# Sigmoid attention and a swish layer on one core: a new order for the opening, new tables for the visits, other cuts at the end

## The chip, the core and the metric

The kernel runs on one NeuronCore of a Trainium2 chip. The core has TensorE (PE: matmuls; its loads of weights are listed apart as PEld), VectorE (DVE), ScalarE (ACT), GpSimd (POOL) and SyncE (SP). Here GpSimd issues the loads (and does a few products), SP issues the first loads and all stores. The metric is the time of one execution on the device, in microseconds; the time before is a median of three runs. All other times are counted from the start of the profiled span.

## The reference

The inputs are `q`, `k`, `v` of shape (8, 12, 448, 64), `w_in` (768, 2048), `w_out` (2048, 768) and `beta` (2048).

```python
scores = matmul(q, k.transpose(0, 1, 3, 2)) / sqrt(64) - log(448)
attn   = 1 / (1 + exp(-scores))                  # a sigmoid, no softmax
x      = matmul(attn, v)                         # to (8 * 448, 12 * 64) = (3584, 768)
h      = x @ w_in                                # (3584, 2048): "first layer"
g      = h / (1 + exp(-beta * h))
out    = g @ w_out                               # (3584, 768): "second layer"
```

## The kernel before, in words

**Groups and visits.** The 12 heads of a batch form three groups of four (`g` = 3 * batch + group; 24 in all). A group's q and k are loaded as fp16 and transposed on VectorE (`transpose`, L208 for q, L217 and L221 for k). A visit (`visit`) is the scores of one group against 128 keys: 8 matmuls of 448 columns (`score`, L237) into two PSUM score tiles of two banks each, then one sigmoid over all four banks on ScalarE (`weigh_two`, L265). The 64 keys left over of two groups share one visit, with 16 matmuls. So the next visit's scores wait until ScalarE has read all four banks. `attend` ("values", L340) multiplies the weights by v, and VectorE copies the result to `xTs` (L349).

**Dense work.** `dense1` (L362) is the first layer of batches 0 and 1: six matmuls per 128 hidden columns, a sigmoid with `beta` (L374), a product on VectorE (L377) into `gt`. The later batches go through `blocks` (L531 and others) between the visits of one window and the next. The second layer is `dense2` (L392), `strassen` (L651, on pairs of 128-token tiles, with sums of hidden columns on VectorE, L638, and adds of results, L669) and `single` (L445, one tile alone). These matmuls form one list, `fill`, and are taken from it one after the other.

**Order.** Every engine executes in the order in which the kernel writes its instructions (`manual_schedule`). In the opening, the list `BEGIN` sets it item by item: `("scores", g, half, second)` is half a group's queries against two key tiles (`second` 0) or the rest (`second` 1), each with two sigmoids (L250); `("idle", n)` is n matmuls on zeros (L820, 256 columns); `("k", g)`, `("q", g, half)` are transposes; `("v", 0)` doubles the leftover keys' v (L171); `("values", g, half)`; `("beta",)` transposes beta (L834); `("dense", n)` takes n matmuls from `fill`. In this stretch there are three score tiles, from `("two",)` on two. `LOADS` is the order of the loads on GpSimd's queue; `("loads",)` puts the list `LATER` behind it. All later waits in the queue follow this order.

After `BEGIN`, a loop over `visits` follows. Each visit is followed by as many dense matmuls as the rest of the list divided by the visits left, plus `MORE[n]` matmuls for visit n. `LATE[n]` says behind how many of them the values of the group before come. Visit 0 is the first of group 3.

**The end.** The last tile of 128 tokens is done alone: its right half of 384 columns first (L445, copied by VectorE, L413), then the left half in two pieces of `QUART` = 192 columns, 16 matmuls each; ScalarE copies each piece (L407) and SP stores it (L703). `store` cuts the stores of the last batch only at the ends of tiles and of the batch.

Of the kernel before, what the change touches and what calls it, by code (L numbers as in the profile page):

```python
# [13 lines left out]
def kernel(  # L14
# [14 lines left out]
    B, H, S, D = q.shape  # L29
    NTOK, DM = out.shape  # L30
    DFF = moe_w_in.shape[1]
    P = 128
# [12 lines left out]
    HALF = DM // 2  # L45
# [36 lines left out]
    def touch(i: int):  # L82
        used[i] = max(used.values(), default=0) + 1

    def bank(cols: int = S, hold=None, at=None):
        if at is None:
            at = min((i for i in used if i not in held.values()), key=used.get)
        assert at not in held.values()
        touch(at)
        if hold is not None:  # L90
            held[hold] = at
        width[at] = cols
        return ps[:, at, 0:cols]
# [287 lines left out]
    m2s = {}  # L381
    left = {}
    def release(key):
        touch(held.pop(key))
        m2s.pop(key)

    def dense2(t: int, half: int, dc: int):

        if dc == 0:
            m2s[t, half] = bank(HALF, (t, half))  # L390
        m2 = m2s[t, half]
        nc.tensor.matmul(  # L392
            m2,
            gt[:, dc, cols(t)],
            w_out16[:, dc, half * HALF : (half + 1) * HALF],
            start=(dc == 0),
            stop=(dc == NDC - 1),
        )
        if dc == NDC - 1:
            leave(t, half, m2)  # L400

    def leave(t: int, half: int, m2, piece=None):
        lo, hi = half * HALF, (half + 1) * HALF
        if piece is not None:
            release((t, half, piece))
            lo, hi = lo + piece * QUART, lo + (piece + 1) * QUART
            nc.scalar.copy(out=osbs[t][:, lo:hi], in_=m2)  # L407
            store(t, lo, hi)
            return
        release((t, half))  # L410
        if t not in osbs:
            osbs[t] = outp.tile([P, DM], FP32, tag="osb", name="osb")
        nc.vector.tensor_copy(out=osbs[t][:, lo:hi], in_=m2)  # L413
        left[t] = left.get(t, 0) + 1
        if t == NT - 1:
            store(t, lo, hi)
        elif left[t] == 2:
            store(t, 0, DM)

    QUART = HALF // 2  # L420

    def sum_of_halves(t: int):
        sums[t, 0] = sump.tile([P, ND, P], FP16, tag="sum", name="sum")
        nc.vector.tensor_tensor(out=sums[t, 0], in0=hid(t, 0), in1=hid(t, 1), op=ALU.add)

    def single(t: int, n: int, dc: int, piece=None):

        if (n, dc) == (0, 0):
            if (t, 0) not in sums:
                sum_of_halves(t)  # L430
            for half in range(1 + (t < NT - 1)):
                m2s[t, 1 - half] = bank(HALF, (t, 1 - half))
        if piece is not None and (n, dc) == (1, 0):
            m2s[t, 0, piece] = bank(QUART, (t, 0, piece))
        both = sums[t, 0]
        half, x, w = (
            (1, hid(t, 0), B12),
            (0, hid(t, 1), B21),
            (1, both, B22),
            (0, both, B11),  # L440
        )[n]
        m2 = m2s[(t, half) if piece is None else (t, half, piece)]
        stop = n > 1 and dc == ND - 1
        w = w[:, dc] if piece is None else w[:, dc, piece * QUART : (piece + 1) * QUART]
        nc.tensor.matmul(m2, x[:, dc], w, start=(n < 2 and dc == 0), stop=stop)  # L445
        if stop:
            leave(t, half, m2, piece)

    NT = NTOK // P
# [165 lines left out]
    def hid(t: int, half: int):  # L615
        return gt[:, half * ND : (half + 1) * ND, cols(t)]
# [23 lines left out]
    def strassen(t: int, i: int, dc: int):  # L640
# [45 lines left out]
        elif i == 6:  # L686
            add(o1[:, L], a, o1[:, L], ALU.subtract)
            release((t, "a"))
            store(t, 0, DM)

    def store(t: int, lo: int, hi: int):
        osb = osbs[t]
        c, end = t * P, (t + 1) * P
        while c < end:
            b, i = divmod(c, S)
            rows = out[b * S : (b + 1) * S, lo:hi]
            if b == B - 1:
                n = min(end - c, S - i)
                to = rows[i : i + n]
            else:  # L700
                n = BLK
                to = rows.rearrange("(p c) m -> c p m", c=NB)[i // BLK]
            nc.sync.dma_start(out=to, in_=osb[c - t * P : c - t * P + n, lo:hi])  # L703
            c += n
# [10 lines left out]
    def alone(t: int):  # L715
        order = [(n, None) for n in range(4)]
        if t == NT - 1:
            order = [(0, None), (2, None), (1, 0), (3, 0), (1, 1), (3, 1)]
        for n, piece in order:
            for dc in range(ND):  # L720
                yield M2_US, lambda a=(t, n, dc, piece): single(*a), n < 3
# [41 lines left out]
    with tc.manual_schedule():  # L763
        def load(what, *a):
# [15 lines left out]
                load_w_out(*a)  # L780

        LOADS = [
            ("q", 1, 0), ("k", 1), ("k", 2), ("q", 2, 0), ("v", 0, 3), ("last",), ("q", 1, 1), ("q", 2, 1),
            ("q", 0, 1), ("w_in", 0, 2), ("w_in", 2, 4), ("w_in", 4, 6), ("w_in", 6, 8), ("w_in", 8, 10),
            ("w_in", 10, 12), ("w_in", 12, 14), ("w_in", 14, 16),
        ]
        LATER = [
            ("qk", 3), ("w_out", 0, 0), ("w_out", 1, 0), ("values", 1), ("qk", 4), ("qk", 5), ("w_out", 0, 1),
# [27 lines left out]
        idle = bank(512)  # L816
# [13 lines left out]
        def beta_columns():  # L830
# [4 lines left out]

        BEGIN = [
            ("cast", 1, 0, 8, False), ("cast", 1, 8, 14, True), ("cast", 0, 0, 7, True), ("k", 0), ("q", 0, 0),
            ("q", 1, 0), ("idle", 20), ("scores", 0, 0, 1), ("k", 1), ("idle", 1), ("idle", 4), ("idle", 2),
            ("k", 2), ("q", 2, 0), ("scores", 1, 0, 0), ("idle", 9), ("v", 0), ("scores", 1, 0, 1),
            ("scores", 0, 0, 0), ("idle", 7), ("scores", 2, 0, 0), ("values", 0, 0), ("q", 1, 1),  # L840
            ("scores", 2, 0, 1), ("beta",), ("q", 0, 1), ("values", 1, 0), ("scores", 0, 1, 0),
            ("values", 2, 0), ("scores", 0, 1, 1), ("dense", 6), ("scores", 1, 1, 1), ("two",), ("dense", 9),
            ("loads",), ("scores", 1, 1, 0), ("q", 2, 1), ("dense", 21), ("scores", 2, 1, 0), ("dense", 12),
            ("values", 0, 1), ("scores", 2, 1, 1), ("values", 1, 1), ("values", 2, 1), ("dense", 45), ("k", 3),
            ("q", 3, 0), ("q", 3, 1), ("dense", 33),
        ]
        for what, *a in BEGIN:
            if what == "q":
# [44 lines left out]
        def left_us(n: int):  # L893
# [2 lines left out]
        AV_US = 1.5  # L896
        GLANCE = 3
        MORE = {
# [3 lines left out]
        }  # L902
        RESERVE = (1.99, 3.28)
        LATE = {
            0: 1, 17: 1, 26: 6, 34: 4, 45: 2, 48: 3, 68: 10, 72: 10,
        }
        turns = {4 * QPB: 1, 6 * QPB: 1}
        first = [next(i for i, x in enumerate(visits) if x[0] == g) for g in range(QPB, NQUAD)]
# [118 lines left out]
```

## Time and profile before

| what | us |
|---|---|
| median of 3 runs (lowest, highest) | 374.64 (374.45, 375.24) |
| the profiled execution: time, span | 374.53, 372.8 |
| busy: TensorE | 366.1 |
| busy: ScalarE | 260.0 |
| busy: VectorE | 254.4 |
| last matmul ends / last copy ends / last store issued | 369.5 / 369.9 / 370.2 |

The busy time of TensorE contains matmuls that overlap, with modelled ends, and the 43 matmuls on zeros; starts of matmuls tell more than ends. In a row of the timeline, the two numbers are start and length, both in microseconds, of consecutive instructions of one kind (x says how many), and the bracket holds the engine's idle time just before and what ended it. In the waits of an engine, the three numbers are the total in microseconds, how often, and the longest. In the chain, a share is part of the span of the work that ended last, followed back.

### The profile page before, as it was taken

Reading aid. Unit: us, or ns where it says so; the run is one execution under the profiler, and the core shown is the slowest. Engines: PE = TensorE matmul, PEld = TensorE weight load, DVE = VectorE, ACT = ScalarE, POOL = GpSimd, SP = SyncE. Lnnn points to the kernel's source line nnn. Section 1 sums busy time; section 2 is a strip of 40 time slices with the busy share of each in tenths; the row PEclk is TensorE's granted clock in tenths of the full one; section 3 lists DMA queues with packets and bytes.
Section 4 is the critical chain, followed back from the end, with each engine's and each line's share of the span. In section 5 each row is a group of like instructions: output and inputs, shape, how many; then the busy total and the mean of one; then the engine's idle time right before and its main releaser. Section 6 shows DMA issues by size and latency. Waiting matters only on the chain.

```text
span 372.8 us, 7315 instructions
## 1 busy us (share of the span) xinstructions
PE 366.1 (98%) x2907; PEld 185.1 (50%) x2907; DVE 254.4 (68%) x479; ACT 260.0 (70%) x311; POOL 90.4 (24%) x136
## 2 busy tenths in 40 slices
PE   8899999999999999999999999999999999999996
PEld 5466544443444455544444445554444455555664
DVE  4335786776586966787666767778767667679671
ACT  5995766698967668887777749887678647883000
POOL 7833343141151013234133003235100002230000
PEclk9999999999999999999999999999999999999999
DMA  9999999993369030029829410018903111000333
GB/s 171 177 195 203 198 204 198 218 124 51 51 85 174 1 86 1 2 49 128 165 38 218 103 24 21 3 30 113 164 4 86 42 44 42 3 0 1 86 84 128
DMA packets 42546, 34.65 MB, mean 93 GB/s; under 512 B 21888, under 2 KB 38928, under 8 KB 42512
## 3 DMA queue, kind: packets, MB, share of 16 engines
q0 software_dynamic: 36688, 22.47, 44.5%
q1 hardware_dynamic: 5824, 11.71, 10.9%
q8 instruction: 23, 0.38, 0.4%
q14 instruction: 11, 0.09, 0.1%
HBM read 45.62 MB, written 11.01 MB: 152 GB/s over the span
## 4 chain that ended last, share of the span: by engine, by line
PE 89%; ACT 5%; DVE 2%; DMA 1%; issue 1%; POOL 0%; ACTq 0%; POOLq 0%
PE ps L531 26%; PE ps L651 25%; PE ps L237 11%; PE ps L340 10%; PE ps L362 9%; PE ps L392 4%; PE ps L445 4%; ACT attns L265 2%; ACT attns L250 2%; DMA raw<-in_k_dram 1%; ACT sg L374 1%; DVE xT L349 0%; DVE qT L208 0%; DVE kT L217 0%; ACT osb L672 0%
## 5 line engine op out<-in xcount | busy, mean ns | idle before, releaser
L265 ACT ACTIVATE attns<-ps,nlogs 128x1792 f16<-128x1792 f32 x75 | 131.7, 1756 | 41.1 <-PE ps L237 40.1
L651 PEld LDWEIGHTS <-sum 128*128 128x128 f16 x440 | 40.4, 98 | 37.0 <-issue 12.1
L545 POOL TENSOR_TENSOR gt<-attns,sg 128x448 f16<-128x448 f32 x21 | 23.9, 1139 | 141.6 <-ACT sg L542 141.6
L237 PE MATMUL ps<-qT,kT 32*128 32x448 f16 (+3 forms) x864 | 52.3, 341 | 2.1 <-ACT attns L250 1.1
L542 ACT ACTIVATE sg<-ps,beta_sb 128x448 f32<-128x448 f32 x72 | 45.3, 633 | 8.4 <-PE ps L531 5.9
L531 PE MATMUL ps<-xT,w_in 128*128 128x448 f16 x216 | 49.2, 353 | 0.0
L531 PE MATMUL ps<-xT,w_S 128*128 128x448 f16 x216 | 49.2, 352 | 0.0
L651 PE MATMUL ps<-w_T,sum 128*128 128x384 f16 x264 | 48.5, 327 | 0.0
L545 DVE TENSOR_TENSOR gt<-ps,sg 128x448 f16<-128x448 f32 x72 | 44.3, 619 | 3.9 <-ACT sg L542 3.7
L349 DVE CAST xT<-ps 128x448 f16<-128x448 f32 (+1 forms) x54 | 28.9, 568 | 19.8 <-PE ps L340 19.8
L531 PEld LDWEIGHTS <-w_in 128*128 128x128 f16 x288 | 28.0, 98 | 26.6 <-issue 0.7
L340 PE MATMUL ps<-attns,v 128*64 128x448 f16 (+3 forms) x432 | 40.6, 340 | 0.1
L669 DVE TENSOR_TENSOR osb<-ps,osb 128x384 f32<-128x384 f32 x55 | 30.5, 555 | 14.4 <-PE ps L651 12.6
L362 PE MATMUL ps<-xT,w_in 128*128 128x448 f16 (+1 forms) x240 | 39.8, 316 | 0.1
L638 DVE TENSOR_TENSOR sum<-gt 128x1024 f16<-128x1024 f16 x55 | 36.5, 680 | 0.2
L377 DVE TENSOR_TENSOR gt<-ps,sg 128x448 f16<-128x448 f32 (+1 forms) x40 | 20.0, 528 | 22.6 <-ACT sg L374 22.5
L126 POOL DMA_DIRECT2D raw<-in_q_dram x26 | 14.5, 560 | 81.0 <-DVE kT L221 75.1
L651 PE MATMUL ps<-w_out,gt 128*128 128x384 f16 x176 | 33.4, 327 | 0.0
L651 PE MATMUL ps<-w_out,sum 128*128 128x384 f16 x176 | 32.2, 327 | 0.0
L591 DVE TENSOR_TENSOR ps<-ps,attns 128x448 f32<-128x448 f32 x24 | 15.2, 633 | 23.3 <-PE ps L531 20.0
L531 PEld LDWEIGHTS <-w_S 128*128 128x128 f16 x216 | 21.1, 98 | 19.4
L362 PEld LDWEIGHTS <-w_in 128*128 128x128 f16 x240 | 21.9, 98 | 16.8 <-issue 5.6
(54 smaller groups left out, 377.0 us busy)
## 6 DMA issues: line engine op xcount, KB each, us to landing
out_dram<-osb SPq DMA_DIRECT2D x100, 96.0 KB, 2.2
raw<-in_k_dram POOLq DMA_DIRECT2D x23, 224.0 KB, 5.6
raw<-in_q_dram POOLq DMA_DIRECT2D x21, 224.0 KB, 3.8
v<-in_v_dram POOLq DMA_DIRECT2D x32, 144.0 KB, 6.2
w_in<-in_moe_w_in_dram POOLq DMA_DIRECT2D x8, 384.0 KB, 10.4
w_out<-in_moe_w_out_dram POOLq DMA_DIRECT2D x4, 768.0 KB, 13.8
v<-in_v_dram POOLq DMA_DIRECT2D x16, 48.0 KB, 6.1
out_dram<-osb SPq DMA_DIRECT2D x2, 384.0 KB, 2.3
```

The lines of the kernel that those rows point to most:

```text
L237: nc.tensor.matmul(sco[base : base + nk, hh, u0 : u0 + n], kT[g][lo : lo + BLK, jt * P : jt * P + nk, e], qT[g][lo : lo + BLK, c0 : c0 + n ...
L265: nc.scalar.activation(out=attns[:, slot : slot + 2].rearrange("p n h s -> p (n h) s"), in_=sco, func=AF.Sigmoid, bias=nlogs[:, 0:1], scal ...
L340: nc.tensor.matmul(av[hh * D : (hh + 1) * D, 0:n], vs[b][base : base + nk, 2 * (s % NPAIR) + hh, jt], at[base : base + nk, hh, 0:n], start ...
L349: nc.vector.tensor_copy(out=xTs[b][:, s % NPAIR, c0 : c0 + n], in_=av[:, 0:n])
L362: nc.tensor.matmul(m1, w_in16[:, hc, dc * P : (dc + 1) * P], xTs[b][:, hc, c0 : c0 + n], start=(hc == 0), stop=(hc == NHC - 1),)
L377: nc.vector.tensor_tensor(out=gt[:, dc, off : off + n], in0=m1, in1=sg[:, 0:n], op=ALU.mult)
L531: nc.tensor.matmul(out, w[:, c, i * P : (i + 1) * P], m[:, c], start=(start and c == 0), stop=(c == KH - 1), skip_group_check=not start,)
L542: nc.scalar.activation(out=sg, in_=h, func=AF.Sigmoid, bias=0.0, scale=beta_sb[:, dc : dc + 1])
L545: return lambda: engine.tensor_tensor(out=gt[:, dc, b % 2 * S : b % 2 * S + S], in0=h, in1=sg, op=ALU.mult)
L638: nc.vector.tensor_tensor(out=sums[t, i], in0=x, in1=y, op=op)
L651: nc.tensor.matmul(m2, (x if op is None else sums[t, i])[:, dc], w[:, dc], start=first, stop=(dc == ND - 1), skip_group_check=i >= 4,)
L669: nc.vector.tensor_tensor(out=out, in0=in0, in1=in1, op=op)
```

## The change

In the opening, the two visits of group 0's first half of queries stand next to each other, with 4 of the matmuls on zeros between them; the later such matmuls are set 2, 2, 8 and 6 (before: 1, 4, 2, 9 and 7). Beta is transposed ahead of the doubling of v instead of after the third group's scores. The loads of v's leftover keys move ahead of group 2's q, group 0's second half of q goes ahead of group 2's, and the last two slices of `w_in` swap. The dense matmuls between the later scores change from 6, 9, 21, 12, 45, 33 to 12, 6, 21, 9, 39, 45; `loads` comes one step later. `MORE` and `LATE` have other entries. At the end the left half is cut into 256 and 128 columns, and the stores of the last batch, but for the last tile, take at most 48 rows.

```diff
-            lo, hi = lo + piece * QUART, lo + (piece + 1) * QUART
+            lo, hi = CUTS[piece : piece + 2]
...
-    QUART = HALF // 2
+    CUTS = (0, 2 * P, HALF)
...
-            m2s[t, 0, piece] = bank(QUART, (t, 0, piece))
+            m2s[t, 0, piece] = bank(CUTS[piece + 1] - CUTS[piece], (t, 0, piece))
...
-        w = w[:, dc] if piece is None else w[:, dc, piece * QUART : (piece + 1) * QUART]
+        w = w[:, dc] if piece is None else w[:, dc, CUTS[piece] : CUTS[piece + 1]]
...
+    ROWS = 48
+
     def store(t: int, lo: int, hi: int):
...
-                n = min(end - c, S - i)
+                n = min(end - c, S - i, P if t == NT - 1 else ROWS)
...
         LOADS = [
-            ("q", 1, 0), ("k", 1), ("k", 2), ("q", 2, 0), ("v", 0, 3), ("last",), ("q", 1, 1), ("q", 2, 1),
-            ("q", 0, 1), ("w_in", 0, 2), ("w_in", 2, 4), ("w_in", 4, 6), ("w_in", 6, 8), ("w_in", 8, 10),
-            ("w_in", 10, 12), ("w_in", 12, 14), ("w_in", 14, 16),
+            ("q", 1, 0), ("k", 1), ("k", 2), ("last",), ("q", 2, 0), ("v", 0, 3), ("q", 1, 1), ("q", 0, 1),
+            ("q", 2, 1), ("w_in", 0, 2), ("w_in", 2, 4), ("w_in", 4, 6), ("w_in", 6, 8), ("w_in", 8, 10),
+            ("w_in", 10, 12), ("w_in", 14, 16), ("w_in", 12, 14),
         ]
...
         BEGIN = [
             ("cast", 1, 0, 8, False), ("cast", 1, 8, 14, True), ("cast", 0, 0, 7, True), ("k", 0), ("q", 0, 0),
-            ("q", 1, 0), ("idle", 20), ("scores", 0, 0, 1), ("k", 1), ("idle", 1), ("idle", 4), ("idle", 2),
-            ("k", 2), ("q", 2, 0), ("scores", 1, 0, 0), ("idle", 9), ("v", 0), ("scores", 1, 0, 1),
-            ("scores", 0, 0, 0), ("idle", 7), ("scores", 2, 0, 0), ("values", 0, 0), ("q", 1, 1),
-            ("scores", 2, 0, 1), ("beta",), ("q", 0, 1), ("values", 1, 0), ("scores", 0, 1, 0),
-            ("values", 2, 0), ("scores", 0, 1, 1), ("dense", 6), ("scores", 1, 1, 1), ("two",), ("dense", 9),
-            ("loads",), ("scores", 1, 1, 0), ("q", 2, 1), ("dense", 21), ("scores", 2, 1, 0), ("dense", 12),
-            ("values", 0, 1), ("scores", 2, 1, 1), ("values", 1, 1), ("values", 2, 1), ("dense", 45), ("k", 3),
-            ("q", 3, 0), ("q", 3, 1), ("dense", 33),
+            ("q", 1, 0), ("idle", 20), ("scores", 0, 0, 1), ("idle", 4), ("scores", 0, 0, 0), ("k", 1),
+            ("idle", 2), ("k", 2), ("q", 2, 0), ("idle", 2), ("scores", 1, 0, 0), ("beta",), ("idle", 8),
+            ("scores", 1, 0, 1), ("v", 0), ("idle", 6), ("scores", 2, 0, 0), ("values", 0, 0), ("q", 1, 1),
+            ("scores", 2, 0, 1), ("q", 0, 1), ("values", 1, 0), ("scores", 0, 1, 0),
+            ("values", 2, 0), ("scores", 0, 1, 1), ("dense", 12), ("scores", 1, 1, 1), ("two",), ("dense", 6),
+            ("scores", 1, 1, 0), ("loads",), ("q", 2, 1), ("dense", 21), ("scores", 2, 1, 0), ("dense", 9),
+            ("values", 0, 1), ("scores", 2, 1, 1), ("values", 1, 1), ("values", 2, 1), ("dense", 39), ("k", 3),
+            ("q", 3, 0), ("q", 3, 1), ("dense", 45),
         ]
...
         MORE = {
-            0: -2, 2: 1, 3: -1, 5: 1, 10: 1, 13: 1, 14: -2, 15: 1, 16: -1, 17: -2, 19: -1, 20: -2, 24: -1,
-            27: -1, 28: -1, 32: -1, 34: 1, 35: 1, 43: -1, 44: 1, 45: 1, 46: -1, 47: 1, 49: 1, 51: 1, 52: 2,
-            53: -1, 54: 1, 55: 1, 59: 1, 67: -1,
+            0: -1, 2: 1, 3: -4, 8: -3, 9: 1, 10: 1, 12: 2, 13: 1, 14: -2, 15: 1, 16: -1, 17: -2, 19: -1, 20: -2,
+            25: -2, 27: -1, 28: -1, 32: -1, 34: 1, 35: 1, 43: -1, 45: 1, 47: 1, 49: 1, 51: 1, 52: 2, 53: -1,
+            54: 1, 59: 1, 62: 1, 67: -1,
         }
...
         LATE = {
-            0: 1, 17: 1, 26: 6, 34: 4, 45: 2, 48: 3, 68: 10, 72: 10,
+            0: 1, 6: 1, 8: 3, 17: 1, 26: 6, 34: 4, 45: 2, 48: 3, 68: 10, 72: 10,
         }
```

## The prediction

> **What bounds the kernel now.** I read the page's busy row and chain first, then the waits of TensorE, then the timeline of the opening and of the end.
>
> ```profile
> span 372.8 us, 7315 instructions
> PE 366.1 (98%) x2907; PEld 185.1 (50%) x2907; DVE 254.4 (68%) x479; ACT 260.0 (70%) x311; POOL 90.4 (24%) x136
> PE 89%; ACT 5%; DVE 2%; DMA 1%; issue 1%; POOL 0%; ACTq 0%; POOLq 0%
> PE ps L237 <- ACT attns L250: 1.1, 3, 0.6
> PE ps L237 <- DVE qT L208: 0.5, 1, 0.5
> ...
> 6.79 1.53 ACT L250 ACTIVATE attns<-ps,nlogs 128x896 f16<-128x896 f32 x2 [1.72 <-PE ps L237]
> 8.62 8.54 ACT L250 ACTIVATE attns<-ps,nlogs 128x896 f16<-128x896 f32 x10 [0.29 <-PE ps L237]
> 11.48 0.57 PE L237 MATMUL ps<-qT,kT 32*128 32x224 f16 x14 [0.63 <-ACT attns L250]
> 13.49 0.35 DVE L171 COPY v<-v 64x768 f16<-64x768 f16 x1 [3.95 <-DMA v<-in_v_dram]
> 15.63 0.80 DVE L834 STREAM_TRANSPOSE beta_sb<-beta_in 32x32 f32<-32x32 f32 x4
> 16.47 0.41 DVE L208 STREAM_TRANSPOSE qT<-raw 128x224 f32<-128x224 f32 x1
> 16.94 0.58 PE L237 MATMUL ps<-qT,kT 32*128 32x224 f16 x16 [0.46 <-DVE qT L208]
> 17.55 3.41 ACT L250 ACTIVATE attns<-ps,nlogs 128x896 f16<-128x896 f32 x4 [0.40 <-PE ps L237]
> ...
> 368.70 0.82 PE L445 MATMUL ps<-w_out,sum 128*128 128x192 f16 x8
> 369.56 0.32 ACT L407 COPY osb<-ps 128x192 f32<-128x192 f32 x1 [1.00 <-PE ps L445]
> 369.91 0.33 SPq L703 DMA_DIRECT2D out_dram<-osb  x1
> ```
>
> TensorE is busy 366.1 of 372.8 us and carries 89% of the chain; 3.3 us of its idle time lie behind its last matmul (369.5), 3.2 us in the first 30 us, 0.3 us between. So only three things can move the end: the opening, where ScalarE's sigmoids (L250) run from 6.79 us almost without a break and TensorE waits for them; the last piece's matmuls, copy and store; and the visits between, if ScalarE falls behind there. The profiled execution took 374.53 us (372.8 span, 1.7 around it), 0.11 under the median of the runs, 374.64. The sum is made against 374.53.
>
> **The opening, first price.** Back-to-back sigmoids start 0.10 us before the one ahead of them ends (1.01 us long, 0.91 apart), so a gap costs its idle time plus 0.10. Before, ScalarE has three gaps up to 25.9 us: 0.29 (group 1's scores wait for k, landed 7.34), 0.06 at 12.01 (inside the merged row), 0.40 at 17.55. Lost: 0.39 + 0.16 + 0.50 = 1.05 us. The last has a plain cause: the scores at 16.94 need the q of group 0's second half, whose transpose stands behind beta's four (0.80 us) on VectorE.
>
> After, with the same rows laid end to end (a = first sigmoid of a visit, b = second):
> - Group 0's second visit follows its first; k and q are there. TensorE needs the bank of 0a back (6.79 + 1.01, +0.05 as at 11.43 to 11.48): 7.85; from such a resumption to ScalarE's start the trace has 0.53 (11.48 to 12.01): 8.38, and ScalarE could have started at 8.22. Lost 0.16.
> - Group 1's two visits are then ready before ScalarE is (9.97 against 10.19; 12.0 against 12.0). Group 2's first follows a visit whose second sigmoid is a short one (0.63), the case that cost 0.16 at 12.01: 0.16 again, start 13.59 instead of 13.81.
> - values(0,0) at 13.55; the next scores are ready at 15.40, ScalarE at 15.41: nothing lost.
> - Beta now runs at about 10.4, in VectorE's empty stretch ahead of 13.49, so the late q is transposed at 15.6 to 16.0. Its scores (16.17) next wait for a bank (end of 2a, 16.42): ScalarE starts at 17.0 against a possible 16.84. Lost 0.16 instead of 0.50.
>
> Sum 0.48 lost, a gain of 0.57 us, on ScalarE until 25.9 and, since TensorE waits for these sigmoids up to 30.15 (values(2,1)), on TensorE from there. Twelve dense matmuls ahead of group 1's scores and six behind (six and nine before) keep this: up to 25.9 both orders put the same six dense sigmoids on ScalarE, and 48 dense matmuls stand ahead of values(0,1) in both. Of the 23 filler matmuls between scores 22 stay (0.109 us each), in time that ScalarE sets: counted as nothing, covered by TensorE's waits for L250; without that cover the one is worth 0.11. Bounds: 1.05 if every gap closes; 0, or a loss, if v is late (second rival). I take 0.57, since each of its three remaining gaps copies one the trace shows.
>
> **What the loads do.** The GpSimd queue issues a DMA when the one eight ahead of it has landed (6.31 after 6.03, 7.63 after 7.34), and the DMA row is full (9) for eight slices: order decides, not issue time. The two small v loads move ahead of group 2's q and the four big v loads. Before, the big ones landed at 9.84, 10.85, 11.68, 12.49, the small ones at 13.08 and 13.40. Now q lands about 0.9 late (10.0, needed at 12.6), the doubling copy (0.35) leaves the path, and the last big load lands where the last small one did, 13.40, just ahead of its use at 13.55. The second q of group 0 moves one place up (14.25 for 14.80, needed 15.6), group 2's takes its place (needed 23.4). The two last w_in slices swap: the one for columns 12 and 13 lands at 31.45 instead of 29.48, used at 36.9, 5.4 us of cover. The later loads are emitted one step on, behind w_in in the same queue order: nothing. Group 3's transposes come after 87 dense units instead of 93; their scores after 132.
>
> **The visits.** Their scores need all four score banks back: start to start 2.43 us when ScalarE sets it (0.63 to the sigmoid, 1.75, 0.05), as at 174.32 to 176.75 with 11 dense matmuls. TensorE's own time with 11 is 2.37 (0.2 + 0.285 + 10 x 0.1625 + 0.258). So 11 or fewer cost 0.06 or more, 12 nothing. By the order of matmuls, visits 0, 1 and 10 newly sink to this floor (0.05 + 0.06 + 0.04), 25 with one dense and a values (0.085), 44 and 55 with 11 (0.03 + 0.06): 0.32 worse. Visits 24 (12 for 11), 46 (0.085), 62 (0.54 over 2.0, a late sigmoid: 0.14) and half of the 0.11 at 113.85 are better: 0.34. Net nothing; I keep 0.2 each way. The values held back behind three units at visit 8 only change places.
>
> **The end.** 32 matmuls of 192 columns become 16 of 256 and 16 of 128. Starts follow each other 82.4 ns apart at 192 columns, 109 at 256, 162.5 at 384, 189 at 448: columns/2.4 + 2.4. At 128 that is 55.8; 16 x 109 + 16 x 55.8 = 2.64 us, the 32 x 82.4 of before. The copy: 0.320 us at 192 columns and 0.478 at 384, 0.00082 a column, so 0.053 less. The store: 64 KB instead of 96; bounds 0 and 0.24 (192 KB took 2.37 to land, 96 KB 1.63). The hardware queue moved 11.71 MB in 10.9% of 16 engines' span, 288 GB/s, so 32 KB are worth 0.11: taken. The Trainium skill ("DMA: Bandwidth & Descriptors", section "Anatomy of one DMA — SWDGE (gpsimd) path") fits a fixed 2.0 us plus bytes over 436 GB/s, for DMAs of the other queue; by that the store would gain 0.075 and the sum be 373.83. The five more stores (128 rows cut in 48, 48, 32) hold SP 0.42 us each; the two tiles' six are issued by 366.1, the next store is due at 367.5: 1.4 us of cover. Sum of the end: 0.16 gained.
>
> **Sum.** 374.53 - 0.57 - 0 - 0.16 = 373.80 us.
>
> **Rivals.**
> 1. *The 128-column matmuls are paced by their weights.* A load of weights is recorded with 98 ns and starts right as the matmul ahead of it starts. For it: 98 is above 55.8; 16 x 42 = 0.68 us at worst, 374.5. Against it: at 192 columns the next matmul starts after 82 ns, inside that 98, and the rule columns/2.4 + 2.4 still holds there. "TensorE: Matmul & The Clock Gate", section "Back-to-back issue gap", in the Trainium skill states about 81 ns per matmul for streams with weight loads at 128 columns; by that 0.40 is lost, 374.2. The same sentence gives 131 ns at 512 columns, which this trace contradicts (189 at 448).
> 2. *v becomes the wait.* values(0,0) has 0.15 us of spare, and 0.07 more before scores and ScalarE follow. If the last big v load lands at 13.8 to 14.1, as the uneven steps between v landings (0.32 to 1.01) allow, 0.3 to 0.5 of the gain goes: 374.1 to 374.3. It turns into a loss past 14.3.
> 3. *TensorE stays at half pace, the slower case.* The fillers run 213 ns apart until 5.2 and 109 only from 7.04. The new layout has a wait at 7.4 to 7.85 and another at 9.0 to 9.44. If these keep or bring back half pace over a stretch as long as the first (5.8 us), the 1.6 us of score matmuls and 2.0 of fillers in it double; some 1.6 fits into waits, 2.0 is lost: 375.8. It decides from 1.5 us lost on. Against it: the 0.63 wait before 11.48 slowed nothing after it.
>
> **How the numbers follow.** 0.2% (0.75 us) is about what a measurement can tell. Forecast 0.50 (faster, its lower part touching the line), rival 1 0.14 and rival 2 0.22 (both within), rival 3 0.14, with which I also cover a misfit of the visits that I did not see. Range: 0.48 more if all opening gaps close, 0.13 for the store, part of it: 373.2; up to rival 1's worst with some of rival 2: 374.9. Only rival 3 and the extremes lie outside.
>
> **What the new profile should show.** ScalarE's first gap after 8.32 under 0.1 us, no wait for qT at L208, two gaps near 13.6 and 17.0; the first straight run of dense matmuls (84 of them) starting near 30.0 instead of 30.59; waits of TensorE for L250 that stay; the last 16 matmuls 56 ns apart; the last copy 0.27; about the same idle behind the last matmul less 0.16. It is wrong if values(0,0) starts after 13.7, if fillers at 8 to 11 us are 213 apart, or if visits 0 to 3 last longer than 2.45, 2.43, 2.53 and 1.72.

## The result, and the profile after

The changed kernel took 373.55 us (median of 22 runs, 373.08 to 374.60); the kernel before, run beside it, 374.99 (22 runs, 374.41 to 376.85). The ratio is 0.9961, 95% interval 0.9953 to 0.9969: 1.46 us faster. The forecast was 373.8, inside a range of 373.2 to 374.9; the gain over the runs of before is about twice the 0.73 that the sum had.

The profiled execution of the changed kernel took 374.60 us, the slowest of its 22, so its opening shows what can go wrong in the new order rather than what usually happens. For that reason a second profile (373.34 us, of an experiment below that moves one load) stands beside it for the opening.

The page of the changed kernel: span, busy time, chain.

```profile
span 372.8 us, 7320 instructions
PE 365.8 (98%) x2906; PEld 184.4 (49%) x2906; DVE 254.5 (68%) x479; ACT 259.9 (70%) x311; POOL 90.6 (24%) x136
PE 92%; ACT 5%; issue 1%; DMA 1%; DVE 1%; ACTq 0%
```

The waits of TensorE from 6 to 31 us in the same execution:

```profile
PE ps L362 <- DMA w_in<-in_moe_w_in_dram: 0.6, 1, 0.6
PE ps L362 <- DVE gt L377: 0.6, 1, 0.6
PE ps L340 <- issue: 0.6, 1, 0.6
PE ps L237 <- ACT attns L250: 0.4, 1, 0.4
PE ps L237 <- DVE qT L208: 0.3, 1, 0.3
```

Its timeline, ScalarE's sigmoids and what they wait for, then the end:

```profile
6.70 8.68 ACT L250 ACTIVATE attns<-ps,nlogs 128x896 f16<-128x896 f32 x10 [1.25 <-PE ps L237]
7.75 0.57 PE L237 MATMUL ps<-qT,kT 32*128 32x224 f16 x14 [0.36 <-ACT attns L250]
11.61 0.81 DVE L836 STREAM_TRANSPOSE beta_sb<-beta_in 32x32 f32<-32x32 f32 x4
12.45 0.42 DVE L171 COPY v<-v 64x768 f16<-64x768 f16 x1
14.05 0.55 PEld L340 LDWEIGHTS <-v 128*64 128x64 f16 x12 [0.80 <-DMA v<-in_v_dram]
15.75 4.99 ACT L250 ACTIVATE attns<-ps,nlogs 128x896 f16<-128x896 f32 x6 [0.37 <-PE ps L237]
21.56 0.73 PE L362 MATMUL ps<-xT,w_in 128*128 128x224 f16 x6 [0.58 <-DVE gt L377]
24.24 1.81 PE L362 MATMUL ps<-xT,w_in 128*128 128x224 f16 x15 [0.62 <-DMA w_in<-in_moe_w_in_dram]
26.62 1.75 ACT L265 ACTIVATE attns<-ps,nlogs 128x1792 f16<-128x1792 f32 x1 [0.57 <-PE ps L237]
...
369.45 0.61 PE L445 MATMUL ps<-w_out,sum 128*128 128x128 f16 x8
370.10 0.27 ACT L407 COPY osb<-ps 128x128 f32<-128x128 f32 x1 [0.52 <-PE ps L445]
```

The chain now lies on TensorE for 92% (89% before), and of the old waits the one for group 1's k and the late one for group 0's second q are gone. ScalarE runs ten sigmoids in a row from 6.70. Two breaks are new in kind: 0.37 before 15.75, where v landed late (the row of the weight loads at 14.05 names it; TensorE's list calls the same idle time "issue"), and 0.57 before 26.62, where the scores came late because TensorE waited for a slice of w_in. (The wait for qT of 0.3 that is left belongs to the very first scores, at 5.94; the profile of before has none there, the four profiles of its variants below have 0.35 to 1.06.) The wait for `gt` before 21.56 is new as well, and is in all nine profiles of the new opening: the six dense matmuls behind group 1's scores follow twelve instead of nine. ScalarE has no gap from it in any of them. At the end the last piece has 128 columns, and its copy lasts 0.27 in place of 0.32.

ScalarE in the opening of the second profile, in which nothing lands too late:

```profile
6.67 13.63 ACT L250 ACTIVATE attns<-ps,nlogs 128x896 f16<-128x896 f32 x16 [1.25 <-PE ps L237]
20.19 0.79 ACT L374 ACTIVATE sg<-ps,beta_sb 128x224 f32<-128x224 f32 x2
20.85 1.55 ACT L250 ACTIVATE attns<-ps,nlogs 128x896 f16<-128x896 f32 x2
```

All sixteen sigmoids stand in one row of the timeline; the kernel before had three rows, with 0.29 and 0.40 between them.

To compare profiles, the span is cut at two places: the start of the straight run of dense matmuls (the first L362 of 448 columns) and the start of TensorE's last matmul. "First" is the first sigmoid's start, "opening" the stretch from there to the straight run.

| profile | first | straight run | opening | straight run to last matmul | last matmul to end |
|---|---|---|---|---|---|
| before, 374.53 us | 6.79 | 30.59 | 23.80 | 338.69 | 3.48 |
| after, 374.60 | 6.70 | 31.21 | 24.51 | 338.63 | 2.99 |
| after, run again, 374.18 | 6.87 | 30.68 | 23.81 | 338.62 | 3.01 |
| after, one load moved, 373.34 | 6.67 | 29.93 | 23.27 | 338.63 | 3.00 |

The start of the straight run in the first, second and fourth of them:

```profile
30.59 0.74 PE L362 MATMUL ps<-xT,w_in 128*128 128x448 f16 x3
31.21 0.74 PE L362 MATMUL ps<-xT,w_in 128*128 128x448 f16 x3
29.93 0.74 PE L362 MATMUL ps<-xT,w_in 128*128 128x448 f16 x3
```

So the end gave 0.47 to 0.49 and the middle 0.06 to 0.07 in every one of them; the rest of the 1.46, some 0.9, must come from the opening, although the two profiled executions of before and after, taken alone, show it 0.7 *longer*. The experiments are about these three numbers.

### The profile page after: what moved, and what is told of

It is laid out like the page before. It is cut to its first block, busy times and chain, and to the rows that moved or that the text cites. A ratio compares the mean times of both kernels' runs of the same rounds, so it can differ in the third digit from the quotient of the medians.

```text
span 372.8 us, 7320 instructions
## 1 busy us (share of the span) xinstructions
PE 365.8 (98%) x2906; PEld 184.4 (49%) x2906; DVE 254.5 (68%) x479; ACT 259.9 (70%) x311; POOL 90.6 (24%) x136
## 4 chain that ended last, share of the span: by engine, by line
PE 92%; ACT 5%; issue 1%; DMA 1%; DVE 1%; ACTq 0%
PE ps L651 27%; PE ps L531 26%; PE ps L237 11%; PE ps L340 10%; PE ps L362 9%; PE ps L392 4%; PE ps L445 4%; ACT attns L250 3%; DMA gt<-in_k_dram 1%; ACT attns L265 1%; ACT sg L374 1%; DVE gt L377 0%; DVE kT L217 0%; ACT raw L806 0%; ACT osb L672 0%
## 5 line engine op out<-in xcount | busy, mean ns | idle before, releaser
L362 PE MATMUL ps<-xT,w_in 128*128 128x448 f16 (+1 forms) x240 | 39.9, 316 | 1.2 <-DMA w_in<-in_moe_w_in_dram 0.6
L362 PEld LDWEIGHTS <-w_in 128*128 128x128 f16 x240 | 21.8, 98 | 18.0 <-issue 5.4
```

The source lines that it names most:

```text
L362: nc.tensor.matmul(m1, w_in16[:, hc, dc * P : (dc + 1) * P], xTs[b][:, hc, c0 : c0 + n], start=(hc == 0), stop=(hc == NHC - 1),)
```

## The experiments

They ran in three sets of four, each beside executions of the kernel before on the same chip, with medians of that of 375.08 (the end's first three and the changed kernel run again), 375.02 (tables, loads, beta) and 375.01 (114 DMAs, the two with k later, the step further). Each expectation names its own theories.

### The end: one part at a time

*The end alone, put into the kernel before.* The cuts (0, 256, 384) and the stores of 48 rows; opening and tables as before.

```diff
-    QUART = HALF // 2
+    CUTS = (0, 2 * P, HALF)
...
-                n = min(end - c, S - i)
+                n = min(end - c, S - i, P if t == NT - 1 else 48)
```

> The kernel before with the new end alone: the last left half cut at 256 of 384 columns, and stores of at most 48 rows (112 DMAs on SP's queue instead of 107). Theory A (the end pays through SP's last waits: SP waits for its eight DMA semaphores in a fixed order and the last store now has the last of them, so that nothing is left to look at once it has landed): from the last copy's start to the end of the span 2.70 us instead of 3.24, 0.05 of it the copy, 0.11 the store's landing, about 0.35 the waits after it; the time 0.5 to 0.6 below the kernel before. Theory B (my prediction: copy and store alone): 0.16 below. The opening and the visits as in the kernel before, in both.

Measured: 374.65 us, ratio 0.9986 (0.9977 to 0.9994), that is 0.5 us faster. From last matmul to end: 3.00, as in the changed kernel; from the start of the last copy 2.74, against 3.20 before and 2.70 expected. That is theory A.

*The stores of 48 rows alone.* Last pieces of 192 columns as before; only the second pair of lines above.

> The kernel before with the 48-row stores alone, the cut still 192 and 192 columns: the same stores as before behind 366.1 us, only their number on SP's queue is 112 instead of 107. Theory A (the order of SP's last waits): one wait instead of six between the last store's landing and SP's drain, 0.3 to 0.4 us less from the last copy to the end of the span, the time 0.3 to 0.4 below. Theory B (number of stores plays no part): the time as before within 0.1, six waits after the landing.

Measured: 374.71 us, ratio 0.9991 (0.9981 to 1.0002). The time alone does not decide, the profile does: last matmul to end 3.17 against 3.48. So 0.31 of the 0.48 comes from five more stores. The cut ones are issued 6 us and more before the end and have nothing to do with the last piece.

*The end undone in the changed kernel.*

```diff
-    CUTS = (0, 2 * P, HALF)
+    CUTS = (0, HALF // 2, HALF)
...
-                n = min(end - c, S - i, P if t == NT - 1 else ROWS)
+                n = min(end - c, S - i)
```

> The changed kernel with the end of the kernel before (192 and 192 columns, whole stores, 107 DMAs on SP's queue): the opening and the tables alone. Theory A: 0.85 to 0.95 us below the kernel before, 0.5 to 0.6 above the changed kernel, the six waits after the last landing back. Theory B: 0.16 above the changed kernel, so 1.3 below the kernel before, and the opening alone is worth twice the 0.57 us of the prediction. A rival: the new tables lose or win some tenths in the visits; then the stretch from the first straight dense matmuls to the last matmul differs from the 338.7 us of the kernel before by more than 0.1.

Measured: 373.99 us, ratio 0.9965 (0.9952 to 0.9978); last matmul to end 3.47. The changed kernel, run again beside it, took 373.60.

> The changed kernel once more, for a second profile: the first one was of an execution at the upper end of its times, in which the first k landed at 4.33 us instead of 3.95 and the w_in slices up to 3 us later. Theory A (the late loads of that execution, not the order, held the opening back): with loads landing as in the kernel before, the straight run of dense matmuls starts near 30.0 us, no wait for w_in, the span near 371.7. Theory B (the new order of the loads makes them land later in every execution): first k again near 4.3, w_in waits again, the start of the straight run near 31.2.

Measured: ratio 0.9959 (0.9946 to 0.9972). The difference of the medians, 0.39, agrees with the 0.47 of the profiles, but the two intervals overlap, so the profiles carry this. Of the two theories about the opening neither holds whole: the first k landed at 4.09, the straight run began at 30.68 instead of 30.0, and TensorE waited once more for w_in, 0.58 us. Late loads are part of the slow opening of the profile after, and the order is not rid of the wait for w_in.

*Why five early stores shorten the end.* Behind its last store SP looks at nine semaphores one after the other, one look of 0.028 us every 0.06 us when it need not wait, and then begins to close the kernel. Starts of these looks in the trace, with the landing of the last store (all in us; the bar is the landing):

```
before, 107 DMAs on SP:          370.29 370.35 370.42 | 371.56 371.62 371.68 371.74 371.80 371.86, drain 371.92   landed 371.54
stores of 48 rows, 112 (after):  370.77 370.84 370.90 370.97 371.03 371.09 371.15 371.34 | 371.93, drain 372.00   landed 371.91
```

With 107 DMAs six looks follow the landing, with 112 only one: 0.38 and 0.08 us from landing to drain. The instructions of the trace name the semaphores: SP's DMAs use eight of them in turn (101, then 112 to 118), in all fourteen profiles, and the looks ask for 101, 112, 113 and so on to 118, always in this order. 107 leaves 3 when divided by 8, so the last store has the third, 113, and five more looks follow the one that waited for it; 112 leaves nothing, so the last store has the last, 118, and no look follows its own. A theory that fits two numbers needs a third: the changed kernel with the first half of the last tile cut at 48 rows too, 114 DMAs, remainder 2.

```diff
-                n = min(end - c, S - i, P if t == NT - 1 else ROWS)
+                n = min(end - c, S - i, P if t == NT - 1 and hi - lo < HALF else ROWS)
```

> The changed kernel with the first half of the last tile's store cut at 48 rows too: 114 stores and loads on SP's queue instead of 112, all computed values the same. Theory A (at the end SP looks at its semaphores in a fixed order, and the place of the last store in that order, which goes by the number of DMAs modulo 8, sets how many looks follow its landing): 114 leaves a remainder of 2, so some five to seven looks of 0.06 us follow; last landing to drain 0.35 to 0.45 us instead of 0.08, last copy to the end of the span 3.0 to 3.15 instead of 2.74, time +0.3 to +0.4 (374.0). Theory B (the number plays no part; the shorter tail of the change comes from the smaller last store alone): 2.74 and 373.6 stay, +-0.1.

Measured: 374.41 us, ratio 0.9988 (0.9979 to 0.9996), 0.8 over the changed kernel's 373.6. The looks:

```
114 DMAs on SP:  369.79 370.67 | 371.00 371.06 371.12 371.18 371.25 371.30 371.37, drain 371.43   landed 370.98
```

Seven looks after the landing, 0.45 us, as theory A has it. But the last copy to the end took 3.72, not 3.0 to 3.15: a miss of 0.6. The timeline of this kernel's end shows where it lies.

```profile
367.31 2.43 SPq L705 DMA_DIRECT2D out_dram<-osb  x3
368.29 0.22 PE L445 MATMUL ps<-w_out,sum 128*128 128x128 f16 x1
368.55 0.27 ACT L407 COPY osb<-ps 128x128 f32<-128x128 f32 x1 [0.52 <-PE ps L445]
```

Three stores stand in that row. The first, the third part of the half tile, kept SP for 1.49 us (367.31 to 368.81) where others take 0.42; the store of the 256 columns, whose copy ended at 368.02, was issued at 368.91 and the last one at 369.37. So SP's queue is free of charge only while the next store is not yet due. The changed kernel cuts only the tiles before the last one, has issued their stores some 1.2 us before the next is due, and is not hurt. Why that one store took 1.49 us stays open. All fourteen profiles have single stores of 0.6 to 2.4 us at some places, most often near 118, 135, 196 and 348 us.

### The opening: what group 1's k is worth

Ten profiles were at hand by then, and in them group 1's k landed anywhere from 7.32 to 8.41 us. In the old order of the opening the straight run began 23.24 us behind that landing, each time: 7.34 to 30.59, 7.53 to 30.77, 7.65 to 30.89. The profile of before has the earliest landing of the three, so the old order is usually worse off than its profile tells. To test it, one load was moved, the same in both kernels: group 2's first q ahead of group 1's k.

```diff
-            ("q", 1, 0), ("k", 1), ("k", 2), ("q", 2, 0), ("v", 0, 3), ("last",), ("q", 1, 1), ("q", 2, 1),
+            ("q", 1, 0), ("q", 2, 0), ("k", 1), ("k", 2), ("v", 0, 3), ("last",), ("q", 1, 1), ("q", 2, 1),
```

> The kernel before, with group 2's first q loaded ahead of group 1's k instead of behind group 2's k, so that this k lands later. Theory A (in the old order of the opening the end follows the landing of group 1's k one for one: the straight run of dense matmuls starts 23.24 us behind that landing in three profiles, 7.34 to 30.59, 7.53 to 30.77, 7.65 to 30.89): k lands near 8.3 instead of 7.3 to 7.9, the first gap of ScalarE grows to 1.0 or more, the straight run starts near 31.5, and the median is 0.4 to 0.9 us over the kernel before. Theory B (k's landing is hidden; the three profiles agree by chance): straight run at 30.6 to 31, time within 0.2 us of before.

> The same move of one load in the changed kernel. Theory A (group 0's second visit, which needs no new k, stands in front of group 1's and covers its k until about 8.4): half or less of what the same move costs the kernel before, a gap of ScalarE ahead of group 1's first sigmoids of 0 to 0.5 us, time 373.6 to 374.1. Theory B (the new layout gains only by the gaps that the old one had within its order, and is as exposed to k): the same cost as in the kernel before, 374.0 to 374.5.

Measured: in the kernel before 375.41 us, ratio 1.0030 (1.0004 to 1.0056); in the changed kernel 373.34, ratio to the kernel before 0.9956 (0.9944 to 0.9968), no different from the 0.9961 without the move. ScalarE in the old order with the load moved:

```profile
6.58 1.53 ACT L250 ACTIVATE attns<-ps,nlogs 128x896 f16<-128x896 f32 x2 [1.25 <-PE ps L237]
9.07 8.54 ACT L250 ACTIVATE attns<-ps,nlogs 128x896 f16<-128x896 f32 x10 [0.96 <-PE ps L237]
18.01 3.41 ACT L250 ACTIVATE attns<-ps,nlogs 128x896 f16<-128x896 f32 x4 [0.40 <-PE ps L237]
```

There k landed at 7.80 and the straight run began at 31.03, again 23.23 later: theory A. The landing was earlier than the 8.3 expected, and so were the straight run (31.5 expected) and the gap (0.96 for 1.0 or more), but the rule held. In the changed kernel k landed at 8.54, later than in any other profile, and the row shown above has no break at all: group 0's second visit covers it. So the new place of that visit is worth more than the gap it closed in the profile of before: it takes the landing of k, which varies by a microsecond between executions, off the path. That is theory A, with even less cost than it allowed.

### The load order and beta

*The old load order under the new opening.*

```diff
-            ("q", 1, 0), ("k", 1), ("k", 2), ("last",), ("q", 2, 0), ("v", 0, 3), ("q", 1, 1), ("q", 0, 1),
+            ("q", 1, 0), ("k", 1), ("k", 2), ("q", 2, 0), ("v", 0, 3), ("last",), ("q", 1, 1), ("q", 2, 1),
...
```

> The changed kernel with the loads in the order of the kernel before (v's small loads behind the big ones, group 2's q ahead of both, w_in in its own order). In the three traces with the new order group 1's k landed at 8.17 to 8.41 us, in the three with the old one at 7.34 to 7.65, and the third to fourth w_in slice 0.6 to 1.6 later too. Theory L (the new order of the loads is a cost that the adjoining visits of group 0 hide in part): k of group 1 back at 7.3 to 7.7, the fourth w_in slice before 24.3, no wait of TensorE for w_in, the straight run of dense matmuls from about 30.0; the time 0.2 to 0.5 below the changed kernel. Theory M (the order is a gain: the doubling of v is off the path): values of group 0 wait for the doubled v at 13.8, ScalarE has a gap of 0.2 to 0.4 more near 15.6, the time 0.2 to 0.4 above the changed kernel.

Measured: 373.91 us, ratio 0.9972 (0.9960 to 0.9984), against 0.9959 and 0.9961 for the changed kernel; the intervals overlap, so the load order is worth a few tenths at most, perhaps nothing. Theory L does not fit: k, the fourth slice of w_in (24.85) and the straight run (30.51) came later than it said, and TensorE waited for w_in. Theory M is not shown either: its gap of 0.2 to 0.4 near 15.6 was 0.04. k landed at 8.07 with this old order and at 7.32 in the next experiment with the new one: the spread of its landing does not come from the order of the loads behind it.

*Beta where it was, in the changed kernel; and beta early, in the kernel before.*

```diff
-            ("idle", 2), ("k", 2), ("q", 2, 0), ("idle", 2), ("scores", 1, 0, 0), ("beta",), ("idle", 8),
+            ("idle", 2), ("k", 2), ("q", 2, 0), ("idle", 2), ("scores", 1, 0, 0), ("idle", 8),
...
-            ("scores", 2, 0, 1), ("q", 0, 1), ("values", 1, 0), ("scores", 0, 1, 0),
+            ("scores", 2, 0, 1), ("beta",), ("q", 0, 1), ("values", 1, 0), ("scores", 0, 1, 0),
```

In the kernel before, `("beta",)` moves from there to the place behind `("scores", 1, 0, 0)`.

> The changed kernel with beta's four transposes put back ahead of the transpose of group 0's second q. Theory A (that q's wait cost 0.50 of ScalarE's time and now 0.16): the gap of ScalarE near 17.1 grows from 0.05 to about 0.4, and TensorE waits for that transpose; the time 0.3 to 0.4 above the changed kernel. Theory B (the wait for the bank or for w_in sets this stretch anyway): the straight run of dense matmuls starts where it did within 0.1, the time unchanged.

Measured: 373.90 us, ratio 0.9972 (0.9961 to 0.9982). A gap of 0.51 before 17.28 is back on ScalarE, and TensorE waits for q's transposes again. Its opening lasts 23.59, 0.45 more than the shortest of the new order (23.14, below), which is the growth of that gap. In time the interval overlaps that of the changed kernel: some 0.3, not settled.

> The kernel before with beta's transposes put early (ahead of the doubling of v) and nothing else. Theory A (from the same rows): ScalarE's gap of 0.40 at 17.6 falls to about 0.06, the straight run starts 0.3 to 0.4 earlier for the same landing times of the loads, the time 0.3 to 0.4 below the kernel before. Theory B (the rest of the opening holds the sigmoids back at that place): the gap stays above 0.3, the time within 0.1 of before.

Measured: 374.96 us, ratio 0.9996 (0.9982 to 1.0010), no difference that can be told, although the gap at 17.55 is gone (0.05 in its place, at 19.21). The interval reaches from 0.7 us below to 0.4 above, so the 0.3 to 0.4 of theory A are neither shown nor excluded in the time. The profiled execution took 376.15 and shows something else. TensorE with its granted clock in three stretches of it (the columns: stretch, its length, busy time and count of PE, PEld, DVE, ACT, POOL, then the granted clock, the DMA share and GB/s):

```profile
0.00:8.58 8.58, 5.88 (x43) 3.73 (x44) 2.87 (x9) 4.10 (x6) 6.22 (x16) 1.00 0.82 162
8.58:13.00 4.42, 4.00 (x43) 2.02 (x44) 1.79 (x8) 2.48 (x3) 3.43 (x6) 0.61 1.65 185
13.00:16.00 3.00, 2.51 (x45) 1.67 (x45) 0.35 (x1) 2.95 (x5) 2.96 (x5) 1.00 1.28 175
```

And the start of that stretch in its timeline:

```profile
8.58 0.93 PE L237 MATMUL ps<-qT,kT 32*128 32x224 f16 x16 [1.09 <-DVE kT L217]
9.44 2.10 PE L820 MATMUL ps<-still 128*128 128x256 f16 x9
```

TensorE waited 1.09 us for group 1's k, and then ran the matmuls on zeros 213 ns apart in place of 109: the granted clock was 0.61 on the mean from 8.58 to 13.0. The record of the clock has 0.5 from 8.6 to 12.1 us and 1.0 on both sides, so one stretch of 3.4 us ran at half pace. That is the third rival's mechanism, seen in the *old* order. Two of the 12 runs of the kernel before with the load moved, 379.63 and 379.82, have a granted clock of 0.986 over the whole span where the others have 0.999 or 1.0; two of the 71 runs of the kernel before beside these experiments, 376.50 and 376.91, have 0.994; of its variants, one run with the 48-row stores (376.46, 0.994) and two with beta early (376.15 and 376.36, 0.995). Of the 79 runs of the changed kernel and its variants one has less than 0.998: 0.995, at 374.25. The wait for k does not always bring it: in the profile of the moved load it was 1.06 us, and the nine matmuls on zeros behind it ran 109 ns apart. From 5.2 to 8.6 us, the 3.4 us ahead of the fall, TensorE was busy 1.89 us with beta early and 1.98 with the moved load: so close together lie a fall and none. These executions move no median, but they are the upper tail of the kernel before.

### The tables of the visits

```diff
-            0: -1, 2: 1, 3: -4, 8: -3, 9: 1, 10: 1, 12: 2, 13: 1, 14: -2, 15: 1, 16: -1, 17: -2, 19: -1, 20: -2,
+            0: -2, 2: 1, 3: -1, 5: 1, 10: 1, 13: 1, 14: -2, 15: 1, 16: -1, 17: -2, 19: -1, 20: -2, 24: -1,
...
-            0: 1, 6: 1, 8: 3, 17: 1, 26: 6, 34: 4, 45: 2, 48: 3, 68: 10, 72: 10,
+            0: 1, 17: 1, 26: 6, 34: 4, 45: 2, 48: 3, 68: 10, 72: 10,
```

(The rest of both old tables too.)

> The changed kernel with the two tables of the kernel before for the visits. From the first straight dense matmul to the last matmul of all the kernel before takes 338.67 to 338.70 us, the changed one 338.60 to 338.63. Theory A (the tables shift matmuls between visits and win some hundredths): 338.6 to 338.8, the time within 0.2 of the changed kernel. Theory B (the new opening needs the new tables: with the old ones visits sink below what ScalarE can follow): 338.9 or more, the time 0.3 or more above the changed kernel.

Measured: 374.21 us, ratio 0.9981 (0.9972 to 0.9989), 0.6 slower than the changed kernel. From the straight run to the last matmul 339.06 against 338.63. The new tables gain next to nothing over the kernel before (338.69); they win back 0.43 that the old ones lose behind the new opening, which leaves 45 dense matmuls instead of 33 behind group 3's transposes. With the old tables visit 3 is 0.48 longer (2.25 for 1.77), which the next ten visits win back; the loss that lasts comes in steps behind that, and what brings each step was not followed. This profile also has the cleanest opening: gaps of 0.055, 0.057 and 0.056 and 23.14 us from the first sigmoid to the straight run.

### A step further

18 and 12 dense matmuls instead of 21 and 9 around the last scores but one of group 2, and a last piece of 96 columns.

```diff
-    CUTS = (0, 2 * P, HALF)
+    CUTS = (0, 288, HALF)
...
-            ("scores", 1, 1, 0), ("loads",), ("q", 2, 1), ("dense", 21), ("scores", 2, 1, 0), ("dense", 9),
+            ("scores", 1, 1, 0), ("loads",), ("q", 2, 1), ("dense", 18), ("scores", 2, 1, 0), ("dense", 12),
```

> The changed kernel with two more steps of the same kind: 18 dense matmuls ahead of group 2's last scores but one and 12 behind instead of 21 and 9, and the last piece cut to 96 columns (288 and 96 instead of 256 and 128). If late slices of w_in hold TensorE up at 26 us (gap of ScalarE 0.53 at 26.1 and 0.57 at 26.6 in two profiles of the changed layout), scores that come three matmuls earlier take part of that gap: 0 to 0.4 us less. The last 16 matmuls 42.4 ns apart by columns/2.4 + 2.4, the last copy 0.027 shorter, the last store 0.05 earlier: tail 2.66 for 2.74 after the copy's start. Together 373.2 to 373.6. Against it: at 96 columns the weight loads could set the pace after all (56 or more ns apart, +0.2), and sigmoids moved forward leave a gap later: 373.6 to 373.9.

Measured: 373.53 us, ratio 0.9961 (0.9949 to 0.9973): the same as the changed kernel. The last 16 matmuls start 42.5 ns apart, so weight loads do not set the pace even there; last copy to end 2.70 for 2.74. The copy gave its 0.027, but the store nothing: it landed 1.55 us behind its copy, as with 128 columns (1.55). What the first edit is for did not occur in the profiled execution, where the fourth slice of w_in landed at 23.62. No variant here is shown to beat the changed kernel.

## Why the prediction was right, and where it was not

**The time and the gain.** The time came out within 0.25 us of the forecast, and part of that is luck: the gain was twice the sum's, and the sum started from an execution 0.46 us below the larger sample's median of before. The two errors work against each other. The direction was right, and the gain lies in the opening and at the end, as forecast; both were put too small.

**The end was mis-sized: 0.16 forecast, 0.48 measured.** Its own terms held. The last copy: 0.053 less forecast, 0.27 for 0.32 measured. The store: 0.11 forecast, and the landing came 1.66 and 1.55 us behind the end of the copy. The matmuls of 128 columns: 55.8 ns forecast, 55 to 56 measured. What failed is the step in which five more stores on SP's queue were set against 1.4 us of cover and so counted as nothing. They were hidden where they stand; but the number of DMAs sets how many looks SP still has to make after the last landing, and that is 0.31 us on the path in every profile: 0.38 from landing to drain in the four with 107 DMAs, 0.08 in the nine with 112. The profile of before held the fact: six looks between 371.54 and the drain at 371.92, in the 3.3 us that I left as one lump.

**The opening within its order: 0.57 forecast, 0.66 measured** (23.80 before against 23.14 in an undisturbed profile of the new order). The three gaps that were to be left are there, 0.055 to 0.057 long, near 8.6, 13.8 and 17.2 in that profile, so ScalarE's 0.48 lost is right to about 0.01; the last 0.09 was not followed. The gap after the first visit, 0.056, lies at 8.29 in the profile after, as forecast.

**The opening between executions was left out.** The sum was made on one execution with k at 7.34. The four profiles of the old order and the old loads have it at 7.34, 7.53, 7.65 and 7.92, 7.61 on the mean, and each tenth costs a tenth: 0.27 more for the kernel before, nothing for the changed one. The median of before came out 0.46 above its profiled execution, in 22 runs instead of three; the 0.27 would be part of that, and the rest was not traced. The other way, the new order has waits that the forecast did not have. Together: openings of 23.80, 24.25 and 24.09 in the old order, and of 24.51, 23.81, 23.32, 23.14, 23.15 and 23.18 with the changed kernel's opening and loads (the last with 18 and 12 dense matmuls for 21 and 9); the medians differ by 0.84, against about 0.91 that the end and the visits leave of the 1.46. These are few profiles, so the 0.84 is a rough figure. Where an opening of the new order is longer than 23.14, its gaps on ScalarE tell most of it: the one of 23.81 has a gap of 0.53, 0.63 with the overlap, the one of 23.32 a gap of 0.07, 0.17 with it.

**v and w_in.** The second rival, v as the new wait, is seen: in the profile after, the last of v's first loads landed at 13.99, values(0,0) began at 14.08, and the gap of 0.37 that follows costs 0.47, inside the 0.3 to 0.5 that the rival gave for 13.8 to 14.1. With a landing at 13.89 another profile lost only 0.17 (a gap of 0.07, and 0.10 for the overlap). Six of the nine profiles of the new order have the landing under 13.8, so it is a tail and not the rule. The sign that I set, values(0,0) after 13.7, came up in five of the nine, but two of these have no gap on ScalarE behind it, because their first sigmoid started late too (6.87 and 7.02): the sign should have been counted from the first sigmoid. The wait for w_in I missed, by a step that counted too coarsely: "48 dense matmuls stand ahead of values(0,1) in both". True, but the new list puts 39 instead of 36 ahead of group 2's last scores but one, and numbers 37 to 39 are the first to need the fourth slice of w_in. Its landing at 25.02 in the second profile of the changed kernel shows it:

```profile
22.59 1.90 PE L362 MATMUL ps<-xT,w_in 128*128 128x224 f16 x18
25.07 0.46 PE L362 MATMUL ps<-xT,w_in 128*128 128x224 f16 x3 [0.58 <-DMA w_in<-in_moe_w_in_dram]
25.46 0.58 PE L237 MATMUL ps<-qT,kT 32*128 32x224 f16 x16
```

Three matmuls wait, the scores behind them come late, and ScalarE stands for 0.53. At 24.29 and earlier there is no such gap. In the profile after it is the third slice, landed at 24.20, that TensorE waits for. For the swap of the last two slices and for group 0's q no wait shows, as forecast. (The page's DMA row is full for nine slices, not the eight that I read; nothing hangs on it.)

**The visits: net nothing forecast, 0.07 gained.** Visits 0 to 3 last 2.43, 2.43, 2.56 and 1.77 us; my limits were 2.45, 2.43, 2.53 and 1.72, so two of them were passed, by 0.03 and 0.05, and the sign named there came up without a loss in the whole. This step does not say that the tables are idle: without them the new opening loses 0.43.

**The first rival** (128-column matmuls paced by their weights) is refuted by the 55 to 56 ns. The Trainium skill's 81 ns in "TensorE: Matmul & The Clock Gate", section "Back-to-back issue gap", does not hold in these traces; its rule of columns/2.4 plus about 2.5 ns, in the section "Wait — 56ns, not 53.3ns?" of the same page, does, down to 42.5 ns at 96 columns.

**The third rival** (half pace) did not come in the new order's profiles: the matmuls on zeros between 8 and 13 us run 109 ns apart there. It is seen in the old one; of the new order one run, 374.25 with a granted clock of 0.995, may have had it, without a profile. The Trainium skill, in "TensorE: Matmul & The Clock Gate", section "What's actually happening", has the clock fall after an idle window of about 3.4 us, and a window that runs freely. The length agrees with the stretch of 3.4 us at 0.5 here; but TensorE was far from idle in the 3.4 us before it, and 1.09 us of waiting was enough in one execution where 1.06 was not in another. Which of the rest of the load in that window decides was not tried.

## What to carry to other kernels

Look at what lies between the last landing and the end of the span instruction by instruction: here 0.3 us hung on the number of DMAs that a queue had issued, and a store cut in pieces well ahead of the end changed it. Before a gap is priced from one profile, ask what ended it; if a landing ended it, its spread over executions belongs to the price, and an order that covers the landing gains more than the gap. And when matmuls are moved across a step, count which data the moved ones are the first to need.

## What was not expected of the hardware

- SP looks at its semaphores at the end in a fixed order, nine looks 0.06 us apart. With 107, 112 and 114 DMAs on its queue, six, one and seven of them came after the last landing (0.38, 0.08 and 0.45 us to the drain). Its DMAs use eight semaphores in turn, in all fourteen profiles, so the DMA's number modulo 8 sets its place in that order; other numbers than these three were not tried.
- The load of group 1's k landed between 7.32 and 8.54 us in fourteen profiles, though all that is issued ahead of it, but for one load in two of them, is the same.
- The granted clock of TensorE fell to 0.5 from 8.6 to 12.1 us, behind a wait of 1.09 us, in an execution that had run at full pace since 5.2 us.
- Below some size a smaller store did not land sooner: 64 KB landed 1.55 to 1.58 us behind the end of their copy, 48 KB 1.55 (one profile), 96 KB 1.65 to 1.66.
